# Scores of eight heads in one pass with a running maximum, and more pauses ahead of the products with the exponentials

## The chip, the cores and the metric

The kernel runs on one core of one Trainium2 chip. The metric is the device time of one execution in microseconds (us). A core has five engines with a queue each: TensorE (PE, matrix products, with PEld for its weight loads), VectorE (DVE), ScalarE (ACT), GpSimd (POOL) and SyncE (SP, which issues most transfers). An engine works off its queue in order and waits at an instruction whose inputs are not there.

## The reference

Three stages follow each other on 8 batches of 576 tokens with 512 channels (8 heads of 64).

```python
p_packed = sm_attn(p, k, v)          # 32 packed queries per head look at 576 keys
out = sm_attn(q, p_packed, p_packed) # 576 queries look at 32 packed keys
# second stage: mixing by Fourier transforms, then a dense layer for every token
u = x + real(fft(fft(x, axis=1), axis=2)); un = normalized(u)
x = u + relu(un @ w_ch1) @ w_ch2
# third stage: each token goes through one of eight experts
out[b, s] = p[e] * (relu(x[b, s] @ w1[e]) @ w2[e])
```

`sm_attn` is the usual attention: scores times 1/8, minus the row's greatest score, exponential, divided by the row's sum, times the values. The change touches the first attention (32 packed queries against 576 keys) of each batch.

## The kernel before, in words

**Three parts.** `attention(0)` runs first by itself. Then come the "mixes", the dense layers of the second stage: one for each batch (512 tokens) and two half mixes (R0, R1, 256 tokens) for the tokens left over. Last are the expert blocks (`e1`, `e2`). A mix has 16 steps f. `mm1(f)` (L741) makes a block of hidden activations in 12 matmuls of 512 columns; `mm2(f)` (L761) multiplies one back in 12 more. `mm2` trails `mm1` by two steps, so the last two `mm2` of a mix stand behind the first two `mm1` of the next.

**Attention beside the mix.** `attention(b + 1)` is a generator, and each `yield` is a pause. It is put on a list, with a rate of ATT_RATE steps per tick, when mix b has issued its first two steps; a quarter of a tick passes after each fourth part of an `mm1` or `mm2`, so a mix has 32 ticks and 28 are left for the generator. What remains is drained before the next mix. The generator of a batch has 61 steps, 67 for batches 3 and 7. Beside it run the generators of the weights' conversion (`ch_weights` in the first mix, `expert_weights` from the second on) and of the logits (`after_mix`).

**What sets the order.** The program's order gives each instruction a priority; a planner that knows estimated times then issues, for every engine, the first one that is ready by these estimates. `tc.high_priority(offset=SOON)` moves what stands in it 200 places ahead. The order of each queue is fixed when the program is built. On the chip an instruction that is late holds up all behind it on its engine.

**The first attention of a batch, before.** It goes by halves of the heads (hf = 0, 1; four heads each). Queries are 128 rows, 32 for each of four heads. The keys are cut in two (i = 0, 1; 288 columns).
- `scores(hf)` (L370): for each i four products of 64x32 queries and 64x288 keys in f32, one per head, on a quarter of the array's columns each; each product is two records in the trace. They fill two PSUM tiles of the two that attention has for everything (`psA`). Then the load of v (L331) is issued into the buffer that the half's keys leave.
- `greatest(hf)` (L377 to L379): maximum of both tiles, and minus an eighth of it.
- `exps(hf)` (L384): exponentials with that bias, and their sums.
- `turn(hf)` (L390 to L393): two f16 parts of the exponentials (ACT, then DVE), and a transposing transfer (`et<-ehl`) by SP's queue.
The six steps are scores 0; maximum 0; exponentials 0 and scores 1; turn 0 and maximum 1; exponentials 1; turn 1. Scores, maxima and exponentials have the priority SOON.

After them come the reciprocal of the sums (L403 to L405), and for each half v's two f16 parts (L416 on ACT, L418 on DVE), the load of q (L336) and 30 products `pps` (L429) of the turned exponentials with v. `own` is a mask that picks for each head its own 64 columns of the product. Later steps make the channel products `gp` (L471) whose parts DVE writes (L476), the second attention (L489 to L546, with the slow operation L534), the products with the transforms, and the normalization (L691 on DVE, L696 on POOL) with the transposing transfers `ut<-unh` (L698) that the batch's mix reads.

Of the kernel before, what the change touches and what calls it, by code (L numbers as in the profile page):

```python
# [159 lines left out]


PASS = ((0, 0), (0, 1), (1, 0))
ATT_RATE = 2.3
URGENT = 100
EW_RATE = 1.3
EWS = 2
# [5 lines left out]
SOON = 200  # L172
# [7 lines left out]
def _build(tc, nc, ctx, A, stop):  # L180
    LN16 = math.log(16.0)
# [9 lines left out]
    ap = actx.enter_context(tc.tile_pool(name="ap", bufs=1, side="left"))  # L191
# [123 lines left out]
    def attention(b):  # L315
        count = [0]

        def att(nm):
            count[0] += 1
            if b == 0 and count[0] % 3:  # L320
                return psO.tile([128, 512], F32, tag="o", name=nm)
            return psA.tile([128, 512], F32, tag="att", name=nm)
# [35 lines left out]
        if b == 0:  # L358
            for hf in range(2):
                load_v(hf)  # L360
        s1, mxs, e32s = {}, {}, {}

        def scores(hf):
            s1[hf] = [att(f"s1_{b}_{hf}_{i}") for i in range(2)]

            for i in range(2):
                for p2 in range(2):
                    for r in range(2):
                        d, row = slice(64 * r, 64 * r + 64), 64 * p2 + 32 * r
                        nc.tensor.matmul(s1[hf][i][row:row + 32, :288], pt[d, 2 * hf + p2],  # L370
                                         kts[hf][d, p2, 288 * i:288 * i + 288], start=True, stop=True)
            (load_v if b else load_q)(hf)

        def greatest(hf):
            mx = mxs[hf] = ap.tile([128, 3], F32, tag="mx", name=f"mx{b}_{hf}", bufs=2)
            for i in range(2):
                nc.vector.tensor_reduce(mx[:, i:i + 1], s1[hf][i][:, :288], axis=AX.X, op=ALU.max)  # L377
            nc.vector.tensor_tensor(mx[:, 2:3], mx[:, 0:1], mx[:, 1:2], op=ALU.max)
            nc.vector.tensor_scalar(mx[:, 2:3], mx[:, 2:3], -0.125, LN16, ALU.mult, ALU.add)  # L379

        def exps(hf):
            e32 = e32s[hf] = ap.tile([128, 576], F32, tag="f32w", name=f"e32_{b}_{hf}", bufs=4)
            for i in range(2):
                nc.scalar.activation(e32[:, 288 * i:288 * i + 288], s1[hf][i][:, :288], AF.Exp, bias=mxs[hf][:, 2:3],  # L384
                                     scale=0.125, accum_out=sums[:, hf, i:i + 1])

        def turn(hf):
            ehl = ap.tile([128, 2, 640], F16, tag="h16", name=f"ehl{b}_{hf}", bufs=5)
            nc.gpsimd.memset(ehl[:, :, 576:], 0.0)
            nc.scalar.copy(ehl[:, 0, :576], e32s[hf])  # L390
            nc.vector.tensor_tensor(ehl[:, 1, :576], e32s[hf], ehl[:, 0, :576], op=ALU.subtract)
# [4 lines left out]
        for steps in (((scores, 0),), ((greatest, 0),), ((exps, 0), (scores, 1)), ((turn, 0), (greatest, 1)),  # L396
                      ((exps, 1),), ((turn, 1),)):
            for fn, hf in steps:
                with tc.high_priority(offset=SOON if fn in (scores, greatest, exps) else 0):
                    fn(hf)  # L400
            yield
        rs = ap.tile([128, 2], F32, tag="rs", name=f"rs{b}")
        nc.vector.tensor_tensor(rs, sums[:, :, 0], sums[:, :, 1], op=ALU.add)  # L403
        nc.vector.tensor_scalar(rs, rs, 16e-9, None, ALU.add)
        nc.vector.reciprocal(rs, rs)  # L405
# [153 lines left out]
        for k, (cs, hf) in enumerate(((0, 0), (0, 1), (1, 0), (1, 1))):  # L559
# [14 lines left out]
            if k == 2:  # L574

                zd = att(f"zd{b}")
                n = 0
# [669 lines left out]
```

## Time and profile before

| | |
|---|---|
| median of 3 runs | 1500.04 us (1494.92 to 1502.70) |
| profiled execution | 1495.18 us |
| its span, first to last instruction | 1493.4 us |
| PE busy | 94% of the span |
| DVE busy | 48% |
| ACT busy | 35% |
| POOL busy | 28% |
| mean granted clock of PE | 0.969 |

A busy share is the mean over stages with different limits. The first 79 us are attention(0) alone; the mixes take the time to about 1030 us, with attention beside them to about 890; then the experts follow. PE's clock has two levels, 1.2 and 2.4 GHz; a granted clock of 1 means the higher one throughout. In the views an arrow `<-` in brackets names what ended a wait.

### The profile page before, as it was taken

The numbers are of one execution on the slowest core, as the hardware profiler recorded it, in microseconds if no ns is written. First come the engines' busy times: TensorE is split into PE (matmuls) and PEld (weight loads), VectorE is DVE, ScalarE is ACT, GpSimd is POOL, SyncE is SP. The second block draws the span as 40 slices with busy tenths as digits, with TensorE's granted clock in tenths as the row PEclk, the third lists the DMA queues.
The fourth block names the chain that finished last, engine by engine and source line by source line (L and its number), as shares of the span: only waits on it lengthen the run. The fifth ranks groups of instructions, "written<-read, shape, count | busy, mean of one in ns | idle before, by whom it ended". The sixth has DMA issues, their size and how long they took to land. (4 is left out here: it accounts for less than half of the span.)

```text
span 1493.4 us, 28983 instructions
## 1 busy us (share of the span) xinstructions
PE 1398.4 (94%) x11340; PEld 823.3 (55%) x11340; DVE 709.6 (48%) x1487; ACT 525.1 (35%) x986; POOL 418.0 (28%) x424
## 2 busy tenths in 40 slices
PE   4598898999999999899999999999899999999996
PEld 3334444544564454454444456455677777776764
DVE  5789976566544646655655654523621111111110
ACT  3343354454444545445445444211111111111111
POOL 1412125425421642442443342000211212121211
PEclk6689999999999999999999999999999999999999
DMA  7275475485466647647557455255947636783371
GB/s 272 62 234 175 143 190 156 113 235 154 118 166 178 182 119 203 159 123 224 150 140 197 115 141 163 55 196 148 248 105 235 143 98 164 237 239 71 86 231 51
DMA packets 233165, 239.72 MB, mean 161 GB/s; under 512 B 168191, under 2 KB 179583, under 8 KB 232384
## 3 DMA queue, kind: packets, MB, share of 16 engines
q1 hardware_dynamic: 226464, 217.62, 53.6%
q0 software_dynamic: 6560, 20.19, 4.1%
q8 instruction: 91, 1.49, 0.4%
q14 instruction: 50, 0.41, 0.1%
HBM read 267.38 MB, written 53.74 MB: 215 GB/s over the span
## 5 line engine op out<-in xcount | busy, mean ns | idle before, releaser
L761 PE MATMUL acc<-w2h,ht 128*128 128x512 f16 x1728 | 417.0, 383 | 0.0
L741 PE MATMUL hp<-ut,w1h 128*128 128x512 f16 x1536 | 370.5, 382 | 6.0 <-DMA ut<-unh 5.2
L741 PEld LDWEIGHTS <-w1h 128*128 128x128 f16 x1920 | 183.6, 98 | 186.3 <-issue 19.5
L761 PEld LDWEIGHTS <-ht 128*128 128x128 f16 x1728 | 166.5, 99 | 188.8 <-issue 13.0
L1109 PE MATMUL ehp<-xgt,w1b 128*128 128x128 f16 x3936 | 230.7, 219 | 1.7 <-DMA w1b<-WS 1.2
L1109 PEld LDWEIGHTS <-w1b 128*128 128x128 f16 x3936 | 224.4, 98 | 12.7 <-DMA w1b<-WS 1.4
L308 POOL TENSOR_TENSOR so<-se,so 128x512 f16<-128x512 f32 x128 | 149.3, 1171 | 269.4 <-ACT so L307 251.1
L1127 PE MATMUL eo<-w2b,hx 128*128 128x512 f16 x984 | 219.2, 379 | 0.0
L1117 DVE SCALAR_TENSOR_TENSOR hx<-ehp,hx 128x512 f16<-128x512 f32 x82 | 56.7, 691 | 338.5 <-ACT hx L1116 338.4
L749 DVE SCALAR_TENSOR_TENSOR ht<-hp,ht 128x512 f16<-128x512 f32 (+1 forms) x160 | 101.3, 633 | 142.9 <-ACT ht L748 142.4
L748 ACT ACTIVATE ht<-hp 128x512 f16<-128x512 f32 (+1 forms) x160 | 88.1, 550 | 229.9 <-PE hp L741 229.8
L1127 PEld LDWEIGHTS <-hx 128*128 128x128 f16 x984 | 94.5, 98 | 106.1
L1135 POOL DMA_INDIRECT out<-ys,sidx x41 | 41.6, 1015 | 328.0 <-ACT ys L1134 323.5
L1116 ACT ACTIVATE hx<-ehp 128x512 f16<-128x512 f32 x82 | 48.9, 597 | 181.0 <-PE ehp L1109 176.6
L1134 ACT ACTIVATE ys<-eo,scl 128x512 f32<-128x512 f32 x41 | 28.2, 687 | 179.1 <-PE eo L1127 179.1
L307 ACT CAST so<-se 128x512 f16<-128x512 f32 x128 | 77.8, 615 | 13.0 <-DMA WS<-so 9.8
L306 ACT ACTIVATE se<-se 128x512 f32<-128x512 f32 x128 | 77.5, 622 | 0.2
L1077 POOL DMA_INDIRECT xg<-XS,gidx x41 | 42.2, 1030 | 125.5 <-DVE tfe L1031 53.9
L346 POOL TENSOR_TENSOR qh<-q,qh 128x1420 f16<-128x1420 f32 x12 | 34.6, 2884 | 63.3 <-ACT qh L345 53.3
L741 PE MATMUL hp<-utr,w1h 128*128 128x256 f16 x384 | 47.1, 272 | 0.0
L696 POOL TENSOR_TENSOR unh<-un,unh 128x512 f16<-128x512 f32 x32 | 37.7, 1192 | 21.8 <-ACT unh L695 21.8
L565 PE MATMUL bp<-cst,eh 128*128 128x289 f16 (+1 forms) x192 | 31.8, 305 | 9.8 <-ACT eh L542 6.2
(289 smaller groups left out, 1382.0 us busy)
## 6 DMA issues: line engine op xcount, KB each, us to landing
w1b<-WS SPq DMA_DIRECT2D x156, 512.0 KB
w2b<-WS SPq DMA_DIRECT2D x156, 512.0 KB
se<-in_w SPq DMA_DIRECT2D x64, 512.0 KB
WS<-so SPq DMA_DIRECT2D x128, 256.0 KB
sw<-in_wc SPq DMA_DIRECT2D x32, 512.0 KB
q<-in_qd SPq DMA_DIRECT2D x16, 710.0 KB
v<-in_vd SPq DMA_DIRECT2D x16, 640.0 KB
k<-in_kd SPq DMA_DIRECT2D x16, 576.0 KB
```

The lines of the kernel that those rows point to most:

```text
L306: nc.scalar.activation(st[:, a], st[:, a], AF.Copy, scale=64.0 if k < 4 else 256.0)
L307: nc.scalar.copy(so[:, 0], st[:, a])
L308: nc.gpsimd.tensor_tensor(so[:, 1], st[:, a], so[:, 0], op=ALU.subtract)
L741: nc.tensor.matmul(hp[:, :ntok], w1h[:, f, c, x], ut[:, 4 * y + c, :ntok], start=n == 0, stop=n == 11)
L748: pace[1] = nc.scalar.activation(ht[:, 0, :ntok], hp[:, :ntok], AF.Relu).ins
L749: pace[0] = nc.vector.scalar_tensor_tensor(ht[:, 1, :ntok], hp[:, :ntok], 0.0, ht[:, 0, :ntok], ALU.max, ALU.subtract).ins
L761: nc.tensor.matmul(self.acc[j], ht[:, x, 128 * j:128 * j + 128], w2h[:, f, y], start=f == 0 and n == 0, stop=f == 15 and n == 2)
L1077: nc.gpsimd.indirect_dma_start(out=g_, out_offset=None, in_=XS[0:rows], in_offset=bass.IndirectOffsetOnAxis(ap=gidx[:, b:b + 1], axis=0), ...
L1109: nc.tensor.matmul(hp[:, cols], w1b[b % RB][:, 2 * c + fg, x, cols], xt[b][:, 4 * y + c], start=n == 0, stop=n == 11, skip_group_check=True)
L1116: nc.scalar.activation(ht[:, fg, 0], hp, AF.Relu)
L1117: nc.vector.scalar_tensor_tensor(ht[:, fg, 1], hp, 0.0, ht[:, fg, 0], ALU.max, ALU.subtract)
L1127: nc.tensor.matmul(op, h[:, f // 4, x, 128 * (f % 4):128 * (f % 4) + 128], w2b[b % RB][:, f, y], start=n == 0, stop=n == 23)
```

## The change

For batch 0 the path by halves is kept (`by_halves`). For the others `by_keys` takes its place: the eight heads are scored against the first 288 keys, then against the others. The second group of four heads uses the other column quarter (`r ^ hf`), so that all eight products lie on different parts of the array. The exponentials of the first 288 keys use the maximum so far; when the maximum over all keys is known, they are multiplied by the exponential of the difference. The mask `own` gets a second version for the changed order of the rows. Scores give up the priority SOON for the first product of each group, and the two loads of v come after the second group. The steps are seven instead of six, and each half has two more pauses ahead of its products `pps`: 66 steps instead of 61 (72 instead of 67). ATT_RATE goes from 2.3 to 2.45.

```diff
-ATT_RATE = 2.3
+ATT_RATE = 2.45
...
-    own = ap.tile([128, 128], F16, name="own")
+    own = ap.tile([128, 2, 128], F16, name="own")
     nc.gpsimd.memset(own, 0.0)
     for h in range(4):
-        nc.gpsimd.memset(own[32 * h:32 * h + 32, 64 * (h % 2):64 * (h % 2) + 64], 1.0)
+        for hf in range(2):
+            c = 64 * (h % 2 ^ hf)
+            nc.gpsimd.memset(own[32 * h:32 * h + 32, hf, c:c + 64], 1.0)
...
+        def by_keys():
+            s1, e32s = {}, {}
+
+            mx = ap.tile([128, 5, 2], F32, tag="mx", name=f"mx{b}", bufs=2)
+
+            def scores(i):
+                s1[i] = [att(f"s1_{b}_{hf}_{i}") for hf in range(2)]
+
+                for n in range(8):
+                    hf, p2, r = n // 4, n // 2 % 2, n % 2
+                    d, row = slice(64 * r, 64 * r + 64), 64 * p2 + 32 * (r ^ hf)
+                    with tc.high_priority(offset=SOON if n else 0):
+                        nc.tensor.matmul(s1[i][hf][row:row + 32, :288], pt[d, 2 * hf + p2],
+                                         kts[hf][d, p2, 288 * i:288 * i + 288], start=True, stop=True)
+                if i:
+                    for hf in range(2):
+                        (load_v if b else load_q)(hf)
+
+            def greatest(i):
+                for hf in range(2):
+                    nc.vector.tensor_reduce(mx[:, i, hf:hf + 1], s1[i][hf][:, :288], axis=AX.X, op=ALU.max)
+                if i:
+                    nc.vector.tensor_tensor(mx[:, 1], mx[:, 0], mx[:, 1], op=ALU.max)
+                nc.vector.tensor_scalar(mx[:, 2 + i], mx[:, i], -0.125, LN16, ALU.mult, ALU.add)
+
+            def exps(i):
+                if i == 0:
+                    for hf in range(2):
+                        e32s[hf] = ap.tile([128, 576], F32, tag="f32w", name=f"e32_{b}_{hf}", bufs=4)
+                for hf in range(2):
+                    nc.scalar.activation(e32s[hf][:, 288 * i:288 * i + 288], s1[i][hf][:, :288], AF.Exp,
+                                         bias=mx[:, 2 + i, hf:hf + 1], scale=0.125, accum_out=sums[:, i, hf:hf + 1])
+                if i:
+                    nc.vector.tensor_tensor(mx[:, 4], mx[:, 3], mx[:, 2], op=ALU.subtract)
+                    nc.scalar.activation(mx[:, 4], mx[:, 4], AF.Exp)
+
+            def turn(hf):
+                nc.vector.tensor_scalar(e32s[hf][:, :288], e32s[hf][:, :288], mx[:, 4, hf:hf + 1], None, ALU.mult)
+                turned(hf, e32s[hf])
+
+            for steps in (((scores, 0),), ((greatest, 0),), ((exps, 0), (scores, 1)), ((greatest, 1),),
+                          ((exps, 1),), ((turn, 0),), ((turn, 1),)):
+                for fn, k in steps:
+                    with tc.high_priority(offset=SOON if fn in (greatest, exps) else 0):
+                        fn(k)
+                yield
+            nc.vector.tensor_tensor(rs, sums[:, 0], mx[:, 4], op=ALU.mult)
+            nc.vector.tensor_tensor(rs, rs, sums[:, 1], op=ALU.add)
...
+        yield from (by_keys if b else by_halves)()
...
-            nc.scalar.mul(mrs[:, hf], own, rs[:, hf:hf + 1])
+            nc.scalar.mul(mrs[:, hf], own[:, hf if b else 0], rs[:, hf:hf + 1])
...
             if hf == 1:
                 split_q(0)
+                yield
+            if b:
+                yield
                 yield
```

`turned(hf, e32)` holds the lines of the old `turn`, and `by_halves` the old functions and steps without an edit.

## Rows read from the trace of the kernel before

**Rows 1.** The page's span and busy time of each engine (share of the span).
```profile
span 1493.4 us, 28983 instructions
PE 1398.4 (94%) x11340; PEld 823.3 (55%) x11340; DVE 709.6 (48%) x1487; ACT 525.1 (35%) x986; POOL 418.0 (28%) x424
```
**Rows 2.** Sums by stage: stretch, its us, busy us (instructions) of PE, PEld, DVE, ACT, POOL.
```profile
79.00:196.00 117.00, 107.60 (x640) 53.22 (x639) 105.70 (x208) 46.18 (x89) 19.76 (x22) 0.98 0.60 180
...
300.00:406.00 106.00, 102.53 (x691) 50.98 (x692) 61.98 (x122) 53.29 (x103) 42.51 (x40) 0.98 0.62 168
```
**Rows 3.** Waits of PE by line: us in total, times, longest us.
```profile
PE gp L471 <- DVE g L476: 17.5, 6, 4.5
PE pps L429 <- DMA et<-ehl: 14.1, 3, 9.7
...
PE hp L741 <- DMA ut<-unh: 5.2, 2, 3.6
...
PE pps L429 <- DVE vhl L418: 1.7, 2, 1.0
```
**Rows 4.** PE in order of time, start of mix 2: start us, us, count.
```profile
298.54 0.69 PE L370 MATMUL s<-k,p 64*32 64x288 f32 x8
...
299.60 0.38 PE L741 MATMUL hp<-ut,w1h 128*128 128x512 f16 x1
300.02 0.69 PE L370 MATMUL s<-k,p 64*32 64x288 f32 x8
300.64 1.68 PE L741 MATMUL hp<-ut,w1h 128*128 128x512 f16 x7
302.35 1.17 PE L370 MATMUL s<-k,p 64*32 64x288 f32 x16
303.45 1.04 PE L741 MATMUL hp<-ut,w1h 128*128 128x512 f16 x4
```
**Rows 5.** PE in order of time, what runs between 302.30 and 302.37 us alone.
```profile
302.35 0.45 PE L370 MATMUL s<-k,p 64*32 64x288 f32 x4
```
**Rows 6.** PE in order of time, scores of batch 1 around the first mix's start.
```profile
74.35 1.18 PE L370 MATMUL s<-k,p 64*32 64x288 f32 x8 [9.53 <-DVE ru L650]
...
80.56 2.15 PE L370 MATMUL s<-k,p 64*32 64x288 f32 x16
```
**Rows 7.** Order of time, batch 3: first transposes issued, first products.
```profile
304.30 1.74 SPq L393 DMA_TRANSPOSE et<-ehl  x1
...
327.73 1.03 PE L429 MATMUL pps<-vhl,et 128*64 128x128 f16 x30
```
**Rows 8.** Order of time, batch 4: scores, first transposes, first products.
```profile
465.40 0.69 PE L370 MATMUL s<-k,p 64*32 64x288 f32 x8
...
473.57 4.47 SPq L393 DMA_TRANSPOSE et<-ehl  x1
...
481.25 1.03 PE L429 MATMUL pps<-vhl,et 128*64 128x128 f16 x30 [2.58 <-DMA et<-ehl]
```
**Rows 9.** Line 691, the normalization on DVE: count, shortest/median/longest ns, first and last start.
```profile
L691 DVE TENSOR_SCALAR un<-ul,mv,rstd x16: 542/547/1375, 67.1 to 893.4; 128x512 f32<-128x512 f32 x16
```
**Rows 10.** Order of time, transposes into the mixes' input, and mix 1's first matmuls.
```profile
191.73 2.62 SPq L698 DMA_TRANSPOSE ut<-unh  x2
...
196.36 1.45 PE L741 MATMUL hp<-ut,w1h 128*128 128x512 f16 x6 [1.59 <-DMA ut<-unh]
...
296.27 1.28 SPq L698 DMA_TRANSPOSE ut<-unh  x1
```
**Rows 11.** Order of time, a wait of the channel products: DVE, POOL, PE.
```profile
248.53 3.26 DVE L534 SCALAR_TENSOR_TENSOR eo<-ee,c 99x256 f32<-99x256 f32 x1
250.35 1.15 POOL L308 TENSOR_TENSOR so<-se,so 128x512 f16<-128x512 f32 x1
252.78 0.86 PE L471 MATMUL gp<-cdt,pth 128*64 128x257 f16 x6 [3.78 <-DVE g L476]
```

More of the change, by code (lines that the diff above doesn't have):

```diff
@@ L360, in attention, with turned @@
                 load_v(hf)
[L361 to L387, printed above, removed]
+        rs = ap.tile([128, 2], F32, tag="rs", name=f"rs{b}")
+        def turned(hf, e32):
             ehl = ap.tile([128, 2, 640], F16, tag="h16", name=f"ehl{b}_{hf}", bufs=5)
             nc.gpsimd.memset(ehl[:, :, 576:], 0.0)
-            nc.scalar.copy(ehl[:, 0, :576], e32s[hf])
-            nc.vector.tensor_tensor(ehl[:, 1, :576], e32s[hf], ehl[:, 0, :576], op=ALU.subtract)
+            nc.scalar.copy(ehl[:, 0, :576], e32)
+            nc.vector.tensor_tensor(ehl[:, 1, :576], e32, ehl[:, 0, :576], op=ALU.subtract)
             et = ap.tile([128, 10, 128], F16, tag="h16", name=f"et{b}_{hf}", bufs=5)
@@ L394, in turn @@
             ets.append(et)
[L396 to L403, printed above, removed]
@@ L404, in attention, with by_halves, scores, greatest @@
-        nc.vector.tensor_scalar(rs, rs, 16e-9, None, ALU.add)
-        nc.vector.reciprocal(rs, rs)
+        def by_halves():
+            s1, mxs, e32s = {}, {}, {}
+            def scores(hf):
+                s1[hf] = [att(f"s1_{b}_{hf}_{i}") for i in range(2)]
+                for i in range(2):
+                    for p2 in range(2):
+                        for r in range(2):
+                            d, row = slice(64 * r, 64 * r + 64), 64 * p2 + 32 * r
+                            nc.tensor.matmul(s1[hf][i][row:row + 32, :288], pt[d, 2 * hf + p2],
+                                             kts[hf][d, p2, 288 * i:288 * i + 288], start=True, stop=True)
+                (load_v if b else load_q)(hf)
+            def greatest(hf):
+                mx = mxs[hf] = ap.tile([128, 3], F32, tag="mx", name=f"mx{b}_{hf}", bufs=2)
+                for i in range(2):
+                    nc.vector.tensor_reduce(mx[:, i:i + 1], s1[hf][i][:, :288], axis=AX.X, op=ALU.max)
+                nc.vector.tensor_tensor(mx[:, 2:3], mx[:, 0:1], mx[:, 1:2], op=ALU.max)
+                nc.vector.tensor_scalar(mx[:, 2:3], mx[:, 2:3], -0.125, LN16, ALU.mult, ALU.add)
+            def exps(hf):
+                e32 = e32s[hf] = ap.tile([128, 576], F32, tag="f32w", name=f"e32_{b}_{hf}", bufs=4)
+                for i in range(2):
+                    nc.scalar.activation(e32[:, 288 * i:288 * i + 288], s1[hf][i][:, :288], AF.Exp, bias=mxs[hf][:, 2:3],
+                                         scale=0.125, accum_out=sums[:, hf, i:i + 1])
+            def turn(hf):
+                turned(hf, e32s[hf])
+            for steps in (((scores, 0),), ((greatest, 0),), ((exps, 0), (scores, 1)), ((turn, 0), (greatest, 1)),
+                          ((exps, 1),), ((turn, 1),)):
+                for fn, hf in steps:
+                    with tc.high_priority(offset=SOON if fn in (scores, greatest, exps) else 0):
+                        fn(hf)
+                yield
+            nc.vector.tensor_tensor(rs, sums[:, :, 0], sums[:, :, 1], op=ALU.add)
+            nc.vector.tensor_scalar(rs, rs, 16e-9, None, ALU.add)
+            nc.vector.reciprocal(rs, rs)
@@ new lines, in by_keys, with turn @@
+        def by_keys():
[8 more added lines that the diff above has]
+                        nc.tensor.matmul(s1[i][hf][row:row + 32, :288], pt[d, 2 * hf + p2],
+                                         kts[hf][d, p2, 288 * i:288 * i + 288], start=True, stop=True)
+                if i:
+                    for hf in range(2):
+                        (load_v if b else load_q)(hf)
+            def greatest(i):
[14 more added lines that the diff above has]
+                    nc.scalar.activation(mx[:, 4], mx[:, 4], AF.Exp)
+            def turn(hf):
+                nc.vector.tensor_scalar(e32s[hf][:, :288], e32s[hf][:, :288], mx[:, 4, hf:hf + 1], None, ALU.mult)
+                turned(hf, e32s[hf])
+            for steps in (((scores, 0),), ((greatest, 0),), ((exps, 0), (scores, 1)), ((greatest, 1),),
[6 more added lines that the diff above has]
+            nc.vector.tensor_tensor(rs, rs, sums[:, 1], op=ALU.add)
+            nc.vector.tensor_scalar(rs, rs, 16e-9, None, ALU.add)
+            nc.vector.reciprocal(rs, rs)
@@ L423, in attention @@
                 split_q(0)
+                yield
+            if b:
+                yield
                 yield
```

## The prediction

> **What bounds the kernel now.** I read the page's busy shares first, then the sums by stage, then the list of what TensorE (PE) waited for, and last the order of time around the lines of the change. The reader is to see that PE is busy for 1398.4 of 1493.4 us, so only 95 us are idle [rows 1]. In the stage from 300 to 406 us, one mix with the attention of the next batch beside it, PE is busy for 102.5 of 106 us and VectorE (DVE) for 62; the granted clock is 0.98, the 2.4 GHz level [rows 2]. Only the first mix (79 to 196) is different: DVE is busy for 105.7 of 117 us, and PE is idle for 9 [rows 2]. So the time moves in two ways: by the PE time of what attention(b) issues between the mix's matmuls, and by the waits that stop PE in its order. The largest wait is the channel products' for DVE, 17.5 us; the products with the exponentials (L429) waited 14.1 us for their transposes, most of it (one wait of 9.7) in batch 0, which keeps the old path, and 1.7 for the split of v; the mixes waited 5.2 for their transposed input [rows 3].
>
> **First scores on PE.** Today a batch issues 32 records (16 products, two each) in three groups: 8, 8 and 16. The group of 8 at 300.02 lets the next matmul start at 300.64, 0.62 us later; the 16 at 302.35 take until 303.45, 1.10 us [rows 4]. So 8 more records on the same four tiles cost 0.48, two rounds of 0.24. Entering a group costs about 0.2 more: one matmul of 512 columns starts at 299.60 and the group at 300.02, 0.42 instead of 512 / 2.4 GHz = 0.21 us; seven take 1.71 instead of 1.49 [rows 4]. A batch therefore costs 2 x (0.2 + 0.62) + (0.2 + 1.10) = 2.94 us. The change issues two groups of 16 records on eight different tiles (two row halves by four column quarters). The trace shows four records of four tiles running together: four have started within 0.02 us of the first, and the four end 0.45 us after it [rows 5]. Among them two share each row half. Eight tiles, four on a row half, are not shown, so I bound them. If they all overlap, a group of 16 takes two rounds as the group of 8 does, 0.62 plus a little for issue, 0.66: 2 x 0.86 = 1.72, a saving of 1.2 per batch. If only four overlap, it takes 1.10: 2 x 1.30 = 2.60, a saving of 0.3. A loss I exclude, since the same tiles in the old order give 1.10. I take the full overlap, because the four of rows 5 already mix both kinds of neighbour (same row half, same bank) with no loss. For batches 2 to 7 that is 6 x 1.2 = 7 us, at the low end 2.
>
> A rule speaks against it: the Trainium skill, "TensorEngine Tiling (Array Packing)", Gotcha 1 (PSUM Pressure), says that different row tiles cannot access the same PSUM bank at once, and in the change each of the two banks is written from both row halves. By that rule the eight would run in two turns and the saving would be 2 us instead of 7. This trace does not agree with it for four tiles [rows 5]: they write one bank from both halves. With eight no run here shows it yet.
>
> For batch 1 I take nothing. Its first groups stand where PE waits anyway (9.5 us for DVE before 74.35), and its 16 records at 80.56 take 2.15 us, at half the speed of later ones [rows 6]; afterwards all 32 stand behind the mix's start, 1.7 us at the full clock, 3 at half: between 0.5 less and 1 more.
>
> **Order and pauses.** The old score groups have priority 200 and jump ahead: the first of batch 3 runs at 298.54, before the next mix's first matmul at 299.60 [rows 4]. In the change the first product of each group keeps its place in the program, after four blocks of 12 matmuls (48 x 0.213 = 10.2 us) and most of half a tick. A tick is 106 us / 32 = 3.3 us [rows 2]. So the chain starts about 12 us later. The products of the first half move from the 9th step at 2.3 per tick (3.9 ticks) to the 12th at 2.45 (4.9), those of the second half from the 13th (5.65) to the 18th (7.35): 3.3 and 5.6 us later. In batch 3 today the first transposes are issued at 304.30, 5.8 us after the scores, and the products start at 327.73 [rows 7]: 23 us to spare, less the transfer. In the change the turn of either half needs both key halves: two more rounds of maximum and exponential, about 5 us, so the issue comes some 11 us after the scores, and 12 + 11 leaves about 327.73 + 3.3 - 321.5 = 9.5 us for the transfer. Batch 4 shows how long that can be: its transposes were issued at 473.57, 8.2 us after its scores, and PE waited 2.58 until 481.25, 7.7 after the issue began [rows 8]. 9.5 against 7.7 fits; with batch 4's 8.2 in place of batch 3's 5.8 it would miss by half a microsecond. So of the waits that are left to later batches, 2.6 for transposes and 1.7 for v, I take 3 us off. Both ends: all 4.3 gone, or 2.6 in each of seven batches.
>
> The loads move with it. v of both halves is issued after the second group, for its buffers are freed by it, and both stand behind each other on SyncE's queue. ScalarE's conversion of v is queued behind the exponentials and would hold up the mix's ReLU if v were late; three buffers of hidden activations cover one such delay. The loads of q follow the split of v, one tick later, and SyncE passes the same transfers as before.
>
> **Added operations.** Per batch DVE gets two multiplications of 128x288 f32 and two tiny operations more, less one; ScalarE one tiny exponential; GpSimd (POOL) four memsets at the start, where nothing waits for it. The nearest row to the multiplication is the normalization's, 128x512 f32 with a scalar per row: 0.542 us at best, 1.375 at worst [rows 9]. At half the width: 0.3 to 1.1 us, so 0.6 to 2.2 per batch. With DVE at 62 of 106 us that lies beside PE; at worst it lengthens the chain to the transposes by 2.2, more than the 1.8 between 9.5 and 7.7. In the first mix, where DVE is the limit, it and the later start push attention(1) back, and the next mix already waits for its transposes: they are issued until 194.35, and the first matmul starts 2.0 us later, at 196.36, after 1.59 of idle PE [rows 10]. I add 1.5 us (ends 0 and 4).
>
> In the later mixes the last transposes end their issue at 297.55; with 2.0 for landing that is 299.55, against a first matmul at 299.60 [rows 4, 10]. Nothing is to spare. The 56th of 61 steps becomes the 61st of 66: 24.35 ticks become 24.9, 1.8 us later. The matmuls of the mix before (24 of them stand behind this first one) can be put ahead of it, so I cost this at nothing; without that cover it is 1.8 x 5 mixes = 9 us.
>
> The middle of attention is denser by 6.5%. There the long wait sits: at 252.78 a channel product waited 3.78 us for DVE, which spent 3.26 on one operation of 99x256 that began at 248.53, while POOL ran subtractions, one at 250.35 [rows 11]. I add 1.5 us for density (ends: 10 less if the shift separates these, 5 more). The skill's page "SBUF — State Buffer", Who interferes with whom, says that DVE and POOL share a port pair and the loser waits out the other's whole instruction; the 3.26 us and the range 0.542 to 1.375 agree.
>
> **Sum.** -7 - 3 + 1.5 + 1.5 = -7 us. The profiled execution took 1495.2 us (span 1493.4 and 1.8 around it), so 1488; it is 4.9 faster than the median of the runs shown, 1500.04, and against that the forecast is 1493.
>
> **Rivals.**
> *Everything fits, and the waits go too.* For it: 4.3 us of waits at the products can all go, and a shifted middle may miss POOL's subtractions. Against: the channel waits came six times, so they are no accident of one place [rows 3]. -7 - 4.3 and up to 10 less: 1479 to 1489, say 1487.
> *The eight tiles don't overlap.* For it: no row shows more than four at once. Against: rows 5. -2 - 3 + 3 = -2: 1498.
> *The later chain arrives late (slower).* Place: the first products with the exponentials. Price: the wait of rows 8, 2.6 us, in each of batches 1 to 7 instead of once, 7 x 2.6 - 2.6 = +15.6; with -7 from PE, -1.7 for v and +3 from DVE it is +10: 1510. It decides from where scores to landed transposes take over 20.5 us (11 + 9.5). For it: rows 8 with two multiplications at their worst. Against: the order of PE was itself planned with such delays, and only one of batches 1 to 7 shows a wait for transposes there.
> That the change does nothing is excluded: both the groups and the steps are other ones.
>
> **Chances.** Forecast 0.48 (1486 to 1499); all fits 0.19; no overlap 0.15; late chain 0.18. About 0.5%, 7.5 us, is what a measurement of this kernel can tell from no change, so the line to "faster" is 1492.5, within the forecast. Faster: 0.48 x 0.48 + 0.19 x 0.9 + 0.15 x 0.15 = 0.42 and a little of chance in the runs, 0.43. Slower: most of the late chain, 0.18 x 0.75, and 0.03 from elsewhere, 0.17. Within: 0.40. Range 1480 to 1508: it leaves out about half of the late chain and a tenth below.
>
> **What would show it.** Right: the scores' 16 records take about 0.66 us to the next matmul (1.10 means no overlap); the first group stands some 12 us after the mix's first matmul; the waits of L429's products for transposes and v fall under 2 us in batches 1 to 7; the channel waits stay near 17 us; the mix from 300 to 406 has 1 us less PE time. Wrong: a wait of 2 us or more at the products in most batches, or first matmuls of a mix that wait for their transposes, 1 to 2 us in each.

## The result, and the profile after

| | before | after |
|---|---|---|
| median of 12 runs | 1496.32 us (1492.02 to 1502.70) | 1510.49 us (1506.02 to 1522.79) |
| profiled execution, its span | 1495.2, 1493.4 us | 1509.2, 1507.3 us |
| ratio of after to before | | 1.0095, 95% interval 1.0073 to 1.0118 |

The change is slower by 14 us. 1493 was forecast, with a range of 1480 to 1508, so the range missed too. The forecast counted from a median of 1500.04 in three runs; the twelve give 1496.32, so 7 us of gain were forecast and 14 of loss came. The rival "the later chain arrives late" had named 1510; it had the time, but only a part of the cause, as the experiments show.

The page's span and busy times of after, to set beside [rows 1]:

```profile
span 1507.3 us, 28998 instructions
PE 1398.2 (93%) x11340; PEld 822.7 (55%) x11340; DVE 718.3 (48%) x1508; ACT 525.5 (35%) x993; POOL 426.3 (28%) x428
```

PE is busy as long as before, so all of the 13.9 us of span is idle time: 95.0 us became 109.1. Where PE waits, by line (us in total, times, longest), answering to [rows 3]; L492 is the old L429, L539 the old L476, L841 the logits, L804 the old L741:

```profile
PE pps L492 <- DMA et<-ehl: 22.7, 9, 10.1
PE lp L841 <- DVE g L539: 17.4, 5, 4.2
...
PE gp L534 <- DVE g L539: 8.1, 4, 2.5
...
PE hp L804 <- DMA ut<-unh: 5.7, 2, 3.6
...
PE pps L492 <- DVE vhl L478: 1.3, 1, 1.3
```

The products wait 8.6 us more for their transposes, nine times instead of three. What stood behind DVE's writing of the channel products (g) cost 17.5 us at the channel products and 1.6 at the logits, which use the same two PSUM tiles; now it costs 8.1 and 17.4, 25.5 in all.

By stretches from one mix's first matmul to the next, the 13.9 us (14.0 by rounded numbers) lie so: 0.4 ahead of the first mix, 4.9 in it (117.2 to 122.1), 9.7 in the other mixes (833.7 to 843.4), and 1.0 less in the experts. In those other mixes PE's idle time rose by 10.9 us: 5.5 for transposes (2.6 to 8.1), 7.5 for g (18.0 to 25.5), 2.1 less elsewhere. The scores cost some 4.5 us less there, by their records and the next matmul's start. About 3 us are left, found by subtraction alone; the granted clock over these mixes is 0.98 after and 0.99 before. Two stages of after (stretch, its us, busy us of PE, PEld, DVE, ACT, POOL, then granted clock), answering to [rows 2]:

```profile
79.00:201.00 122.00, 109.27 (x635) 54.25 (x634) 109.03 (x212) 45.51 (x88) 18.50 (x21) 0.96 0.58 173
...
311.00:424.00 113.00, 104.88 (x712) 52.25 (x711) 66.54 (x131) 53.60 (x104) 45.99 (x43) 0.97 0.58 161
```

In the first mix PE and DVE are each busy for 109 of 122 us, and the granted clock went from 0.98 to 0.96.

Now the start of mix 2 with the scores of batch 3 (PE alone, start us, us, count, in brackets the idle time before), answering to [rows 4, 7]:

```profile
311.59 1.67 PE L804 MATMUL hp<-ut,w1h 128*128 128x512 f16 x7
...
323.34 0.71 PE L426 MATMUL s<-k,p 64*32 64x288 f32 x16
323.99 1.47 PE L804 MATMUL hp<-ut,w1h 128*128 128x512 f16 x6
...
326.60 1.19 PE L426 MATMUL s<-k,p 64*32 64x288 f32 x16
...
338.97 1.03 PE L492 MATMUL pps<-vhl,et 128*64 128x128 f16 x30 [1.79 <-DMA et<-ehl]
```

and the transposes on SyncE's queue:

```profile
333.78 1.94 SPq L371 DMA_TRANSPOSE et<-ehl  x1
...
336.91 1.39 SPq L371 DMA_TRANSPOSE et<-ehl  x1
```

The first group takes 0.65 us to the next matmul. The second takes 1.12 in each of batches 2 to 7 (the next matmul is at 327.73). Its two PSUM tiles come free one after the other, when the exponentials of the first group have read them:

```profile
326.36 0.19 ACT L444 ACTIVATION_READ_ACCUMULATOR e<-s,mx 128x1 f32 x1
...
326.84 0.20 ACT L444 ACTIVATION_READ_ACCUMULATOR e<-s,mx 128x1 f32 x1
```

The first two products start at 326.60, 0.05 us after the first of these ends, the other six at 327.09, 0.05 after the second; so it is in all six batches. So the sixteen records don't stand together. The products start 27.4 us after the mix's first matmul, the first scores 11.7: 15.6 us are left to the chain, of which the last 1.8 are waited.

### The profile page after: what moved, and what is told of

Same layout as the page of the kernel before. It is cut to its first block, busy times and chain, and to the rows that moved or that the text cites. A ratio compares the mean times of both kernels' runs of the same rounds, so it can differ in the third digit from the quotient of the medians.

```text
span 1507.3 us, 28998 instructions
## 1 busy us (share of the span) xinstructions
PE 1398.2 (93%) x11340; PEld 822.7 (55%) x11340; DVE 718.3 (48%) x1508; ACT 525.5 (35%) x993; POOL 426.3 (28%) x428
## 5 line engine op out<-in xcount | busy, mean ns | idle before, releaser
L804 PE MATMUL hp<-ut,w1h 128*128 128x512 f16 x1536 | 376.7, 389 | 9.3 <-DMA ut<-unh 5.7
L804 PEld LDWEIGHTS <-w1h 128*128 128x128 f16 x1920 | 185.5, 99 | 196.6 <-issue 25.9
L824 PEld LDWEIGHTS <-ht 128*128 128x128 f16 x1728 | 165.9, 98 | 184.4 <-issue 10.9
L310 POOL TENSOR_TENSOR so<-se,so 128x512 f16<-128x512 f32 x128 | 153.7, 1209 | 364.0 <-ACT so L309 353.5
L804 PE MATMUL hp<-utr,w1h 128*128 128x256 f16 x384 | 47.1, 272 | 0.2 <-DVE ht L812 0.2
L348 POOL TENSOR_TENSOR qh<-q,qh 128x1420 f16<-128x1420 f32 x12 | 34.6, 2885 | 22.5 <-ACT qh L347 22.4
```

The costliest lines, as they stand in the source:

```text
L310: nc.gpsimd.tensor_tensor(so[:, 1], st[:, a], so[:, 0], op=ALU.subtract)
L804: nc.tensor.matmul(hp[:, :ntok], w1h[:, f, c, x], ut[:, 4 * y + c, :ntok], start=n == 0, stop=n == 11)
L824: nc.tensor.matmul(self.acc[j], ht[:, x, 128 * j:128 * j + 128], w2h[:, f, y], start=f == 0 and n == 0, stop=f == 15 and n == 2)
```

## The experiments

Three theories stood at the start. A, the late chain: the first products of the scores come late in the mix, and the transposes after them. B, the first mix: batch 1's attention beside the DVE-bound first mix. C, the work of the path by keys itself. Later a fourth came: the place in the mix at which the rate (ATT_RATE) puts the middle of attention. Every kernel was timed in five rounds beside the kernel before on its chip. Columns: median; ratio to before with its interval; from the profiled execution the waits (us, times) of the products for transposes, those of channel products and logits for g, and the length of the first mix. Some 11 to 13 us of the transposes' waits are batch 0's, in every kernel. The waits are those of one execution, which can lie some 6 us from the median (e10's took 1510.6 us, e6's 1525.0).

| run | median us | ratio | transposes | g | first mix |
|---|---|---|---|---|---|
| before | 1496.3 to 1500.1 | 1 | 14.1, 3 | 19.1, 7 | 117.2 |
| after | 1510.5 | 1.0095 (1.0073 to 1.0118) | 22.7, 9 | 25.5, 9 | 122.1 |
| e1 after, early scores | 1505.6 | 1.0051 (1.0031 to 1.0071) | 11.3, 2 | 27.8, 12 | 117.9 |
| e2 before, late scores | 1505.8 | 1.0045 (1.0025 to 1.0065) | 16.2, 7 | 16.6, 7 | 115.5 |
| e3 after, no pauses, 2.3 | 1532.2 | 1.0231 (1.0204 to 1.0258) | 30.8, 10 | 27.5, 17 | 119.3 |
| e4 before, pauses, 2.45 | 1509.0 | 1.0071 (1.0049 to 1.0092) | 12.7, 3 | 22.0, 13 | 121.4 |
| e5 e3 with early scores | 1521.2 | 1.0145 (1.0126 to 1.0163) | 15.0, 3 | 28.8, 17 | 118.6 |
| e6 e5, order of second group | 1519.5 | 1.0121 (1.0102 to 1.0141) | 14.3, 3 | 29.6, 17 | 120.0 |
| e7 before, 2.45 | 1507.2 | 1.0053 (1.0038 to 1.0068) | 14.2, 3 | 9.9, 4 | 126.9 |
| e8 e4 from batch 2 | 1500.8 | 1.0010 (0.9997 to 1.0022) | 12.1, 3 | 21.6, 12 | 120.0 |
| e9 e1 from batch 2 | 1507.4 | 1.0040 (1.0025 to 1.0054) | 13.6, 3 | 28.8, 11 | 117.3 |
| e10 after from batch 2 | 1516.4 | 1.0117 (1.0095 to 1.0139) | 20.7, 8 | 26.3, 10 | 118.1 |
| e11 e5 from batch 2 | 1519.9 | 1.0133 (1.0111 to 1.0156) | 15.5, 3 | 27.4, 16 | 115.7 |
| e12 after, no multiplication | 1523.4 | 1.0163 (1.0139 to 1.0187) | 19.1, 7 | 28.8, 14 | 127.2 |
| e13 after, 2.3 | 1522.6 | 1.0153 (1.0123 to 1.0183) | 20.7, 8 | 26.6, 12 | 121.9 |
| e14 e1, 2.3 | 1508.2 | 1.0055 (1.0034 to 1.0077) | 11.9, 3 | 26.8, 11 | 117.9 |
| e15 before, 2.38 | 1489.5 | 0.9934 (0.9912 to 0.9956) | 13.9, 3 | 6.0, 6 | 119.3 |
| e16 before, 2.2 | 1514.4 | 1.0110 (1.0084 to 1.0136) | 12.5, 3 | 30.7, 16 | 121.3 |
| e17 e1, 2.6 | 1504.4 | 1.0045 (1.0029 to 1.0061) | 13.2, 3 | 22.1, 13 | 117.6 |
| e18 e5, 2.38 | 1501.0 | 1.0027 (1.0003 to 1.0051) | 13.3, 3 | 16.2, 10 | 119.0 |

**e1 and e2: the late start from both sides.** e1 is after with the priority SOON for every product of the scores; e2 is before without it for the first product of each half, and with v's load as late, from batch 1 on.

```diff
--- after
+++ e1
-                    with tc.high_priority(offset=SOON if n else 0):
+                    with tc.high_priority(offset=SOON):
--- before
+++ e2
+                        with tc.high_priority(offset=SOON if b and (i or p2 or r) else 0):
...
-                with tc.high_priority(offset=SOON if fn in (scores, greatest, exps) else 0):
+                with tc.high_priority(offset=SOON if fn in (greatest, exps) or (fn is scores and not b) else 0):
```

> The changed kernel with one edit: the first product of each score group has the priority SOON too, so the groups jump ahead again. Theory A (the chain to the exponentials' transposes starts too late, and PE then waits at the products with the exponentials): the first group of a batch stands some 10 to 20 us earlier, the waits of these products for transposes in batches 1 to 7 (22.7 less 11.9 of batch 0, about 11 us in the change) fall to 3 us or less, and the time falls by 8 us or more, to 1502 or less. Theory B (the middle is too dense and the pauses too many, whatever starts the chain): the same time as the change within 4 us, and the waits at the channel products and logits for DVE (25 us) stay. Theory C (the added DVE work of the path by keys): no change of time either, with the waits for transposes gone.

> The kernel before with one edit: in batches 1 to 7 the first of the eight products of each half's scores loses the priority SOON (and the load of v behind them), as in the change. Theory A: waits for transposes at the products grow by 5 us or more and the time by 5 to 15 us, to 1501 to 1511, with the steps and the work of before. Theory B and C: within 3 us of before, 1496, since neither the pauses nor the work are changed.

In e1 the waits for transposes of batches 1 to 7 are gone and the ratio falls by 0.0044, 6.6 us of 1498 (by the ratios, since after and e1 were not timed together); those for g stay:

```profile
PE lp L841 <- DVE g L539: 17.3, 5, 4.1
PE pps L492 <- DMA et<-ehl: 11.3, 2, 9.6
PE gp L534 <- DVE g L539: 10.5, 7, 2.5
```

A had expected 8 us or more. But the early start does something else too: it breaks up the first group, of whose eight products four stand ahead of four matmuls of the mix and four behind them. Its scores of batch 3 (PE alone; `issue`: it waited for nothing that the profile shows):

```profile
303.32 0.69 PE L426 MATMUL s<-k,p 64*32 64x288 f32 x8 [0.79 <-issue]
...
304.90 0.69 PE L426 MATMUL s<-k,p 64*32 64x288 f32 x8
...
307.14 1.11 PE L426 MATMUL s<-k,p 64*32 64x288 f32 x16
```

These are the three groups of the kernel before. To the next matmul the scores of batches 2 to 7 take 14.1 us in before, 10.6 in after and 13.0 in e1; e5, e6, e9, e11, e14, e17 and e18, which start as early, have three groups as well (12.4 to 14.7 us). So no kernel here has the early start and the whole saving of the scores, and the late start by itself costs some 2 to 4 us more than such a pair shows. In e2, with nothing of the path by keys, the late start alone costs 7.4 us (1505.8 against 1498.4, timed together), and the waits for transposes rise from three to seven. So A is a cause, of about half of the loss.

**e3 and e4: the two parts by themselves.** e3 is after without the added pauses at rate 2.3; e4 is before with them at 2.45, so the same lines the other way round.

```diff
--- after
+++ e3
-ATT_RATE = 2.45
+ATT_RATE = 2.3
...
-                yield
-            if b:
-                yield
```

> The changed kernel without the two more pauses for each half and with ATT_RATE 2.3. Theory A: the products are planned about 3 us earlier against the same late chain, so the waits for transposes stay or grow and the time is that of the change or up to 6 us more (1508 to 1517). Theory B: the middle has the density of before, so the waits at channel products and logits fall below 20 us and the time falls to 1500 or less.

> The kernel before with the pauses and ATT_RATE 2.45 of the change alone (scores by halves, all with SOON). Theory A: no wait for transposes in batches 1 to 7 and a time of before within 4 us (1492 to 1500). Theory B: 6 us or more above before (1502 or more), with 5 us more of waits at channel products and logits.

Each part alone loses: 33.8 and 10.6 us. Together they lose 14: the parts don't add up, and no theory had expected e3's 1532. In e3 the products wait ten times, 30.8 us, so the pauses do what they are for. But e4 shows that pauses and rate cost the old path 10.6, of which the waits for transposes explain nothing (12.7 us).

**e5 and e6: the path by keys without a late start.** e5 is e3 with SOON as in e1. e6 also turns the heads' order round in the second group, since the PSUM tile that comes free last had its products last.

```diff
--- e5
+++ e6
-                    hf, p2, r = n // 4, n // 2 % 2, n % 2
+                    hf, p2, r = n // 4 ^ i, n // 2 % 2, n % 2
```

> The changed kernel with all scores at the priority SOON, without the added pauses and with ATT_RATE 2.3: the path by keys alone, started as early as in the kernel before. Theory A+B (the late start and the pauses are the two costs, the path by keys itself costs nothing): between 5 us under and 2 us over the kernel before. Theory C (the added DVE operations or the longer chain of the path by keys cost): 4 us or more above before, with waits for the exponentials' transposes in batches 1 to 7 of 3 us or more.

> As the run before it, with one edit: in the second group of a batch the four products of the second half's tile come first. In the change that group took 1.12 us to the next matmul instead of 0.65. If the cause is that its tiles come free one after the other (each when its exponentials are done), all eight now wait for the later one and then run at once: 0.65 to 0.70 us in all batches, and 2 to 3 us less than the run before it in time. If eight tiles with two groups in flight are slower by themselves, it stays above 1 us.

Early scores take 0.0086 of before, 12.9 us, off e3 and the waits for transposes with them, but e5 still stands 21.6 us above before, with 17 waits for g. Of the 23.8 us between the profiled spans 12.5 are idle time of PE in the later mixes, and 6.5 are slower work there (PE busy 813.4 for 807.0 us, granted clock 0.98 for 0.99). The turned order didn't do what it was for: in e6 two products again start ahead of the other six, and the second group takes 1.04 us in four batches of six, as in e5. So it says nothing on the group's cause; the time moved by 0.0024, within the two intervals.

**e7 and e8: the rate, and batch 1.** e7 is before with the rate at 2.45 and nothing else; e8 is e4 with batch 1 left at 2.3 and without pauses.

```diff
--- e4
+++ e8
-            if b:
+            if b > 1:
...
-                bg.append([ga, 0.0, ATT_RATE])
+                bg.append([ga, 0.0, ATT_RATE if b else 2.3])
```

> The kernel before with ATT_RATE 2.45 alone. If the denser steps are what the pauses with their rate cost (10.6 us in the run of both together): 6 us or more above before. If the pauses' place does it: within 3 us of before.

> The kernel before with the pauses and the rate 2.45 for batches 2 to 7 only; batch 1, whose attention stands beside the first mix, keeps its steps. If the cost of the pauses is the lengthened chain of batch 1 (the second mix started 5 us later with them): 4 to 6 us less than with the pauses in all batches, so 3 to 7 above before. If it lies in the later mixes: 9 us or more above before.

The rate alone costs 7.5 us, and a first mix of 126.9 us: there PE was busy for 114.5 us at a granted clock of 0.90, against 107.6 at 0.98 [rows 2]. Without it in batch 1, pauses and rate cost 1.2 us, within 0.5%. This spoke for B.

**e9 to e12: is it batch 1?** e9 to e11 keep batch 1 on the old path at 2.3, without pauses and with the old mask: early scores with pauses, late scores with pauses, early scores without pauses at 2.3. e12 is after without the multiplication.

```diff
--- after
+++ e9, e10, e11
-        yield from (by_keys if b else by_halves)()
+        yield from (by_keys if b > 1 else by_halves)()
...
--- after
+++ e12
-                nc.vector.tensor_scalar(e32s[hf][:, :288], e32s[hf][:, :288], mx[:, 4, hf:hf + 1], None, ALU.mult)
```

> After the change, but batch 1 keeps the path by halves, no added pauses and rate 2.3, and in batches 2 to 7 the first product of each group has its priority back. Theory 'batch 1 and the late start' (the loss of 14 us is batch 1 beside the first mix, plus the late start of the chain): both are gone, the scores' saving of about 4 us is left: 1495 to 1497 us against 1498 before, and no wait of the products for their transposes in batches 1 to 7. Theory 'the path by keys itself costs' (longer chain, later middle, seen without pauses as +16 us at the same early start): 1502 to 1507, with more waits of the channel products for DVE than the six of before.

> The same with the late first products of the change. Theory 'late start': 4 to 6 us above the early one, with waits of the products for their transposes of 1 to 2.5 us in most of batches 2 to 7; theory 'batch 1 alone': equal to the early one within 2 us.

> Path by keys in batches 2 to 7 with early first products, no added pauses and rate 2.3 throughout. If what the path by keys cost without pauses (1521 in all batches) sits in batch 1 beside the first mix, this gives 1496 to 1500; if every batch pays about 3 us for it (a longer chain and a middle that meets the channel products), it gives 1512 to 1518, with 10 or more waits of the channel products for DVE.

> The change without the two multiplications of the first 288 columns by the exponential of the difference of the maxima, so the part of the softmax that brings the first keys to the common maximum is left out. They took 0.37 us each, 0.73 us a batch, in the chain from scores to transposes. If the chain's length decides (late chain), the nine waits for transposes (22.7 us) shrink by 0.4 to 0.7 us each in batches 1 to 7 and the time by 2 to 5 us; if DVE's extra work lies beside PE, the time is the same within 2 us.

B fell. With batch 1 as before, the first mix is as long as before (117.3), and the time is no better than with batch 1 on the new path: e9 1.0040 against e1's 1.0051, e11 1.0133 against e5's 1.0145. e10 against e9 gives the late start again, 9.0 us. e12 shows most: 0.73 us of work a batch taken out of the chain, the waits for transposes 3.6 us shorter, as the late chain wants it, and the time no shorter but well above after's. DVE's queue has another order, most of all in the first mix, where a wait came up that after doesn't have:

```profile
PE bp L627 <- DVE g L538: 4.5, 1, 4.5
```

5.2 of the 9.0 us between the two spans are the first mix, and 4.3 of these are slower work of PE, not waits (busy 113.6 for 109.3 us, granted clock 0.92 for 0.97). Another 4.4 lie in the experts; these take 466 to 467 us in e4, e6, e8, e9, e10 and e12 and 461 to 465 in the others, and why was not looked into.

**e13 to e16: the place of the middle.** Nothing but the number in ATT_RATE: 2.3 in after (e13) and in e1 (e14), 2.38 (e15) and 2.2 (e16) in before.

```diff
--- before
+++ e15
-ATT_RATE = 2.3
+ATT_RATE = 2.38
```

> The change with its pauses and its late first products, but with the rate of before, 2.3. Theory 'the rate' (2.45 moves the middle of attention to where DVE meets POOL and the channel products wait): 1500 to 1505 us, first mix about 117 us, waits of channel products and logits for DVE near 19 us instead of 25. Theory 'the path itself': 1508 to 1515, waits for DVE stay at 25 or more.

> The same with early first products. Theory 'the rate': 1495 to 1500, with no waits for transposes in batches 1 to 7. Theory 'the path itself': 1505 to 1512, since the early start alone gave 1505.6 at rate 2.45.

> The kernel before with nothing but the rate at 2.38, half of the step to 2.45, which alone gave 1507. If the cost grows with the rate: 1501 to 1504. If the place of the middle scatters the time without a direction: anything from 1497 to 1512, with the difference in the first mix and in the waits of the channel products for DVE.

> The kernel before with nothing but the rate at 2.2, below the old one. If the cost grows with the rate: 1494 to 1498. If 2.3 was a low point among scattered places: 1501 to 1512.

The rate of before doesn't bring the time back: e13 and e14 stand at 1522.6 and 1508.2, where the theory of the rate had 1500 to 1505 and 1495 to 1500. The kernel before gives 1514, 1498, 1489.5 and 1507 us at 2.2, 2.3, 2.38 and 2.45: a range of 25 us without a direction, wider than either text had expected. The waits of e15:

```profile
PE pps L429 <- DMA et<-ehl: 13.9, 3, 9.6
...
PE gp L471 <- DVE ee L502: 6.0, 5, 1.4
...
PE gp L471 <- DVE g L476: 5.1, 4, 2.8
```

and those of e16:

```profile
PE gp L471 <- DVE g L476: 22.9, 12, 2.7
PE pps L429 <- DMA et<-ehl: 12.5, 3, 9.6
...
PE lp L778 <- DVE g L476: 7.8, 4, 2.6
```

The transposes are nearly the same; what moves most is g, from 6.0 to 30.7 us (with the logits' 0.9 and 7.8), or from 12.5 to 33.2 with the waits for `ee`. That is not the whole: of the 22.4 us between the two profiled spans 14.6 are idle time of PE in the later mixes and 4.3 slower work there (PE busy 802.3 and 806.6 us, granted clock 1.00 and 0.98); 4.1 lie ahead of and in the first mix. e7 is the exception: 9.9 us of g, and the first mix's 126.9. In mix 2 of e15 the channel products start from 44.7 to 53.1 us after the mix's first matmul, in e16 from 45.1 to 59.7, in before from 43.8 to 55.7, in after from 51.0 to 67.2. The first three begin within 1.3 us of each other, so their place in the mix doesn't tell them apart. What differs is what DVE works on ahead of g while POOL runs. In e16:

```profile
249.49 5.74 DVE L532 SCALAR_TENSOR_TENSOR eo<-ee 128x256 f32<-128x256 f32 x2
...
253.80 1.15 POOL L308 TENSOR_TENSOR so<-se,so 128x512 f16<-128x512 f32 x1
...
255.35 0.41 DVE L476 SCALAR_TENSOR_TENSOR g<-gp,g 128x257 f16<-128x257 f32 x1
...
255.82 0.59 PE L471 MATMUL gp<-cdt,pth 128*64 128x257 f16 x3 [2.70 <-DVE g L476]
```

The second of the two operations starts at 250.01, takes 5.2 us and ends 0.3 us after POOL's last of six operations in a row. The shortest, median and longest of this line in before and in e16:

```profile
L532 DVE SCALAR_TENSOR_TENSOR eo<-ee x16: 409/422/1190, 44.9 to 833.0; 128x256 f32<-128x256 f32 x16
...
L532 DVE SCALAR_TENSOR_TENSOR eo<-ee x16: 409/420/5233, 45.1 to 847.5; 128x256 f32<-128x256 f32 x16
```

Between ACT's reading of a channel product and DVE's (24 in batches 2 to 7) DVE worked on an operation of over 2 us in 2 cases in e15, 5 in before, 10 in e16, and 10 or 11 in e3, e5, e6 and e11. After has only two, so this is not all of its 25.5 us. No run moved POOL's work alone, so what these operations cost of the time is argued, not shown. e15 is the fastest kernel of all. e13 against e14 is the late start once more, 14.4 us:

```profile
PE gp L534 <- DVE g L539: 23.0, 7, 4.0
PE pps L492 <- DMA et<-ehl: 20.7, 8, 11.0
```

against e14's

```profile
PE gp L534 <- DVE g L539: 22.0, 6, 4.0
PE pps L492 <- DMA et<-ehl: 11.9, 3, 10.9
```

**e17 and e18: the path by keys at a place of its own.** Early scores with pauses at 2.6 (e1 with another number), and without pauses at 2.38 (e5 with another number).

> Path by keys with early first products and the pauses, at rate 2.6: the first channel products, 47.0 us after the mix's start at 2.45, come to about 44.5, where they are at rate 2.38 without the new path (1489.5 us). Theory 'place': the waits of channel products and logits for DVE fall from 27 us to under 15, and with the scores' saving of 4 us the time is 1486 to 1495. Theory 'the path itself': 1500 to 1510, waits for DVE over 20 us.

> Path by keys with early first products, no pauses, rate 2.38 (2.3 gave 1521). Theory 'place': the channel products start at 44 to 45 us as in the kernel before at 2.38, and 1488 to 1500 us; theory 'the path itself': 1510 to 1522, since one step and two multiplications more a batch stay.

The rate counts here too: from 2.3 to 2.38 the path without pauses goes from 1521.2 to 1501.0, its waits for g from 28.8 to 16.2 us, and the operations of over 2 us ahead of g from 10 to 3. So most of what e5 seemed to put on the work of the path by keys (theory C) goes with the rate; 3.7 us above before are left. In e17 the channel products of mix 2 start at 45.7 us, about as early as in e16, and g's waits are 22.1: the theory of the place, which had 1486 to 1495 us and under 15 of waits, fails. Neither beats before, nor e15. None of the twelve kernels with the path by keys and its multiplication was faster than before. Whether some rate, or a start that is early and keeps the first group whole, would bring out the 4 us of the scores stays open: at four rates the old path itself spread over 25 us.

## Why the prediction was wrong, by its own steps

**First scores on PE: right for one group of two.** The first group takes 0.65 us (0.66 predicted), so eight tiles do run together. The second takes 1.12, and six batches save about 4.5 us instead of 7. The step assumed that sixteen records of a group are issued together; the second group's two PSUM tiles come free one after the other. The Trainium skill, "TensorEngine Tiling (Array Packing)", Gotcha 1 (PSUM Pressure), says that different row tiles can't access the same PSUM bank at the same time, and had been weighed against this step. In the first group each of the two banks is written from both row halves, and 0.65 us for sixteen records is two rounds of eight: the trace doesn't agree with the rule for these tiles.

**Order and pauses: the step that failed.** It said that the chain starts "about 12 us later" and leaves "about 9.5 us for the transfer". Its measure was 299.60 in [rows 4], taken as the next mix's first matmul. That matmul belongs to the 16th step of the mix before. The next mix starts at the second line here (before, PE in order of time):

```profile
304.32 2.75 PE L761 MATMUL acc<-w2h,ht 128*128 128x512 f16 x12
306.92 2.32 PE L741 MATMUL hp<-ut,w1h 128*128 128x512 f16 x10
```

There are 192 matmuls `hp` in a mix, and counting them from the first one gives it. So the old scores of batch 3 (298.54) stood 8.4 us ahead of the mix, the new ones 11.7 behind its start: a shift of 20.1 us, not 12. What the prediction had right is the rest of the chain: 10.4 us from scores to issue (11 predicted), and from the start of the issue at 333.78 another 5.2 until the products at 338.97 (7.7 in [rows 8]). The products themselves came 4.8 us later in the mix without their wait (from 20.8 to 25.6 us after its start; 3.3 predicted). With 20 in place of 12 the sum gives 9.5 - 8 = 1.5 us for a transfer that takes about 5, so the same sum, rightly anchored, says that the products wait in most batches. The waits came out at 3.0 us in batch 1 and 0.5 to 2.0 in the others, for the most part smaller than the rival's 2.6 each, since the products start somewhat later than its 3.3. Of the prediction's own signs the first group's place came true (11.7 us behind the mix's first matmul, where it had said some 12), for the step counted that place from the right end; what it had wrong was where the old scores and the products stood. Five pairs that differ by the edit of the early or late start price it: 6.6 (after, e1), 7.4 (e2, before), 12.9 (e3, e5), 9.0 (e10, e9) and 14.4 us (e13, e14), always to the same side. In four of them the early kernel has lost 2.3 to 3.7 us of the scores' saving, so the late start costs that much more there. It costs more than the transposes' waits grow (2 to 16 us in these pairs) in three of the five; where the rest lies was not settled.

**The first matmuls of the mixes: right, by a wrong reason.** "Nothing is to spare" rested on the same 299.60; 7 us were to spare, and the waits for `ut` moved by 0.5 us.

**Added operations and density: mis-sized.** The multiplication took 0.37 us, within its ends, beside other work. But 1.5 us for density, with ends of -10 and +5, was meant as the price of one change in one place. g's waits rose by 6.4 us, and the experiments show that these waits alone go from 6 to 31 us with the rate. Here is such a wait in after, in the order of time on all engines:

```profile
368.09 2.98 DVE L591 SCALAR_TENSOR_TENSOR ah<-ee,ah 128x512 f16<-128x512 f32 x1 [0.16 <-issue]
...
368.26 2.27 POOL L607 TENSOR_TENSOR eh<-eo,eh 128x512 f16<-128x512 f32 x2
...
373.25 0.42 DVE L539 SCALAR_TENSOR_TENSOR g<-gp,g 128x257 f16<-128x257 f32 x1
...
373.72 0.17 PE L841 MATMUL lp<-wgh,xt 128*128 128x18 f16 x1 [4.19 <-DVE g L539]
```

ACT had read the channel product by 370.74, but on DVE's queue g stands behind an operation that took 2.98 us while POOL ran, against 0.67 at its shortest, and five more. PE, which runs in order, had the logits next and stood for 4.19 us. The Trainium skill, "SBUF — State Buffer", Who interferes with whom, which the prediction named for the same pair of engines, says that a DVE instruction with two inputs in SBUF contends with a GpSimd instruction that reads SBUF. The 2.98 us against 0.67, ending 0.5 us after POOL's two operations, agree with it.

**Batch 1 and the first mix: mis-sized.** +1.5 with ends 0 and 4; it was 4.9. 2.7 of these are idle time (3.0 of waits for transposes are new in it). The other 2.2 are PE's work between the two marks, where 11 more matmuls `acc` and 16 fewer records of scores fall and the granted clock is 0.97 for 0.98; these were not told apart. It is not the path by keys in batch 1 as such: with the same path but early scores (e1) the first mix has 117.9 us at the same 0.97, so most of it is the late start again. The old path has 119 to 127 at other rates.

**Sum.** -4.5 for the scores (for -7), +5.5 for transposes (for -3), +7.5 for g in the later mixes and +4.9 in the first mix (for +1.5 each), about +3 that only the subtraction gives, -2.1 of other idle time, -0.6 at both ends: +13.9. The chances were off by the same reading: the late chain, which decided "from where scores to landed transposes take over 20.5 us", decides from 12.5 with the right anchor, and its 15.6 stand above that.

What stays open is how the loss divides. From before over e4 and e1 to after it goes +10.6 (pauses and rate), -3.4 (path by keys, early), +6.6 (late start); from before over e5 and e3 it goes by ratios +21.7, +12.9, -20.4. Only the sign of the late start held on every way.

## What to carry to other kernels

Before a position in a trace is called "ahead of" or "behind" a stage, count the stage's instructions from its start: one matmul taken for another moved a chain by 8 us, and with the rival's own prices that turned the forecast's sign. Where PE runs in order and an engine with a slow, contended operation feeds it, as here, a change of the pace or of one small operation can move waits by more than the edit is worth: vary the pace of the kernel before by a few per cent first, to learn how far the time scatters, and compare two versions each at several paces. Here that showed 25 us of scatter and, at rate 2.38, a kernel 0.66% faster (interval 0.44 to 0.88) than the one that the change started from. And look whether an edit that is to move one thing leaves the rest as it was: the early start here undid most of the grouping that the change was made for.

## What was not expected of the hardware

Eight products on eight different tiles of the array, 64 rows by 32 columns each, took 0.65 us for sixteen records, as long as four products took for eight records before (0.62, [rows 4]). In the first mix at rate 2.45 (e7) the granted clock was 0.90 instead of 0.98, and PE's busy time for as many instructions (640, not all the same ones) 114.5 instead of 107.6 us: some 6.9 of that mix's 9.7 us more lie in PE's work, not in waits. In e16 an operation of DVE, 0.41 us at its shortest, took 4.1 to 5.2 us in four cases, and each time it ended 0.3 us after the last of five or six operations that POOL ran one after the other.
